# Keys and gates on one DMA queue, values on a second: a decode attention kernel with two load queues

## The chip, the cores and the metric

The kernel runs on one core of a Trainium2 chip. The metric is device microseconds of one execution, the median of several. The span on a profile page is about 1.8 us shorter than the device time of the same execution.

## The reference, cut to what matters

One new token for each of 4 batches meets a window of 4096 cached keys and values for 8 key/value heads of 128. A gated ReLU layer runs beside it, and a sigmoid gate mixes the two.

```python
k = jnp.repeat(k_cache[:, :, Sk - W:, :], rep, axis=1)      # W = 4096, rep = 4
v = jnp.repeat(v_cache[:, :, Sk - W:, :], rep, axis=1)
scores = jnp.einsum("bhqd,bhkd->bhqk", q, k) * (Dh ** -0.5)
p = _softmax(scores, axis=-1)
o = jnp.einsum("bhqk,bhkd->bhqd", p, v)
a = o.transpose(...).reshape(B, Sq, Hq * Dh) @ wo           # [...]
b = einsum(relu(x @ W_gate) * (x @ W_up), W_down)           # shortened
return g * a + (1 - g) * b                                  # g = sigmoid(sum(x * gate_w))
```

Everything in bfloat16. The data that has to be read is 81.01 MB: 33.6 MB of keys, 33.6 MB of values, 4.2 MB each of query and output weights, 1.8 MB each of gate, up and down weights. Every byte is used once, by few rows of activations.

## The kernel before

The profile calls TensorE PE, VectorE DVE, ScalarE ACT and SyncE, which here only issues DMAs, SP.

The work is cut into 8 sets (a batch and half of its heads). A set needs one K load and one V load of 4.19 MB each, 128 rows of 32 KB. Per set, VectorE transposes K in four blocks (KT) and takes the scores out of PSUM (ESC), TensorE multiplies scores (SC), VectorE transposes the exponents (PT), TensorE does a small product for the row maximum (SW), row sums (RS) and the value product (PV). ScalarE does the exponent (EXP) and the normalisation (NORM). At the end come gate and up products (GU), the down product (FFN), the fold of the heads (OQ) and the output product (WO).

All loads were issued by SP in one order, into four rotating slots (a slot is a buffer that holds one load):

```python
def _dma_order():
    o = [("wq",), ("x",), ("gw",), ("k", 0), ("k", 1), ("v", 0)]
    for s in range(2, NSET):
        o += [("k", s), ("v", s - 1)]
    return o + [("wg",), ("wu",), ("v", NSET - 1), ("wd",)] + [("wo", p) for p in range(len(WO_PIECES))]
```

The order of the engines' work, PE in particular, comes from one list:

```python
    for s in range(1, NSET):
        o += [("KT", s, 0), ("SC", s - 1, 3)] + [...] + [("SW", s - 1)]
        o += [("KT", s, 1), ("PT", s - 1), ("SC", s, 0), ("KT", s, 2), ("SC", s, 1), ("RS", s - 1), ("KT", s, 3)]
        o += [("SC", s, 2)] + [("PV", s - 1)] * (s < NSET - 1)
    s = NSET - 1
    o += [("SC", s, 3), ("SW", s), ("PV", s - 1), ("PT", s), ("RS", s), ("GU",), ("PV", s), ("FFN",), ("OQ", 1)]
    return o + [("WO", p) for p in range(len(WO_PIECES))]
```

The output product waits for its weights, for the folded heads, and for T2, because it accumulates in the PSUM bank that FFN's result was just read from:

```python
            w = [("WO", p), ("T2",)] + [("E", "OQ", g) for g in range(2)]
```

## Time and profile before

| | before |
|---|---|
| time, median of 3 runs | 197.7 us (197.62 to 197.79) |
| span of the profiled run | 196.2 us |
| bytes read, share of 16 DMA engines' span | 81.01 MB, 96.8% |
| VectorE waiting for keys, in all | 26.0 us |
| last output weights waited for until | 193.4 us |

These are lines of the page of the kernel before: two rows of the slices (40 equal slices of 4.9 us, tenths busy and GB/s), the DMA queue, and the chain that ended last.

```profile
DMA  6999999999999999999999999999999999999990
GB/s 220 441 415 428 456 448 441 418 429 428 434 441 434 434 424 434 428 428 428 428 428 428 424 428 428 441 423 441 418 448 428 434 409 440 429 409 419 420 386 30
...
q1 hardware_dynamic: 3904, 81.01, 96.8%
...
DMA 56%; DVE 32%; PE 7%; SPq 2%; issue 1%
```

The DMA engines are busy from the first slice to the last but one. 96.8% of 196.2 us is 189.9 us of packet time per engine, on average. The chain gives VectorE 32%, but VectorE also waits 26 us for keys: it is not the limit.

The next lines are the tail in the timeline of the kernel before. Columns: start in us, busy time in us, engine, line, operation, output and inputs; in brackets the idle time of the engine before it, and what ended that.

```profile
150.41 2.31 DVE L495 STREAM_TRANSPOSE kt<-slots 128x2048 f32<-128x2048 f32 x1 [4.67 <-DMA slots<-in_A_k_cache_dram]
...
169.35 2.00 ACT L603 ACTIVATE pe<-sc,negmax 128x2048 bf16<-128x2048 bf16 x1 [12.83 <-DVE negmax L532]
...
172.74 1.69 PE L314 MATMUL bank<-slots,xT 128*4 128x448 bf16 x32
...
179.24 5.33 PE L314 MATMUL bank<-slots,pT 128*64 128x512 bf16 x32 [4.81 <-DMA slots<-in_A_v_cache_dram]
...
184.50 1.69 PE L314 MATMUL bank<-slots,sc 128*4 128x256 bf16 x28
...
187.83 1.91 PE L314 MATMUL bank<-slots,oq 128*4 128x256 bf16 x32 [0.63 <-ACT oq L586]
190.90 1.04 PE L314 MATMUL bank<-slots,oq 128*4 128x256 bf16 x16 [1.16 <-DMA slots<-in_A_wo_dram]
...
193.42 0.38 PE L314 MATMUL bank<-slots,oq 128*4 128x256 bf16 x4 [0.26 <-DMA slots<-in_A_wo_dram]
```

Read from top to bottom: the keys of the last set (K7) are there at 150.4, its exponent starts at 169.4, gate and up products at 172.7. PV of the last set waits 4.8 us for V7; FFN starts as soon as PV has ended, at 184.5. Half of the 64 output matmuls are done by 189.7. From there on PE waits for output weights. The tail is bound by DMA: PE has slack before each of the last pieces.

### The profile page before, as it was taken

Reading aid. Unit: us, or ns where it says so; the run is one execution under the profiler, and the core shown is the slowest. Engines: PE = TensorE matmul, PEld = TensorE weight load, DVE = VectorE, ACT = ScalarE, POOL = GpSimd, SP = SyncE. Lnnn points to the kernel's source line nnn. Section 1 sums busy time; section 2 is a strip of 40 time slices with the busy share of each in tenths; the row PEclk is TensorE's granted clock in tenths of the full one; section 3 lists DMA queues with packets and bytes.
Section 4 is the critical chain, followed back from the end, with each engine's and each line's share of the span. In section 5 each row is a group of like instructions: output and inputs, shape, how many; then the busy total and the mean of one; then the engine's idle time right before and its main releaser. Section 6 shows DMA issues by size and latency. Waiting matters only on the chain.

```text
span 196.2 us, 1966 instructions
## 1 busy us (share of the span) xinstructions
PE 125.9 (64%) x784; PEld 56.3 (29%) x784; DVE 127.7 (65%) x192; ACT 30.7 (16%) x66; POOL 14.1 (7%) x38
## 2 busy tenths in 40 slices
PE   0029377584964874787589855965696449754964
PEld 0014223131422321242134422422242123322641
DVE  6105969999499819982997299729973996370000
ACT  2003420040131013001300240014001400420100
POOL 7776000000000000000000000000000000000000
PEclk9999759999999998899579969997999996997899
DMA  6999999999999999999999999999999999999990
GB/s 220 441 415 428 456 448 441 418 429 428 434 441 434 434 424 434 428 428 428 428 428 428 424 428 428 441 423 441 418 448 428 434 409 440 429 409 419 420 386 30
DMA packets 3922, 81.14 MB, mean 414 GB/s; under 512 B 572, under 2 KB 584, under 8 KB 968
## 3 DMA queue, kind: packets, MB, share of 16 engines
q1 hardware_dynamic: 3904, 81.01, 96.8%
q8 instruction: 6, 0.10, 0.2%
q14 instruction: 4, 0.03, 0.0%
q10 hardware_dynamic: 8, 0.00, 0.0%
HBM read 81.01 MB, written 0.00 MB: 413 GB/s over the span
## 4 chain that ended last, share of the span: by engine, by line
DMA 56%; DVE 32%; PE 7%; SPq 2%; issue 1%
DMA slots<-in_A_k_cache_dram 47%; DVE kt L495 21%; DMA slots<-in_A_wo_dram 9%; PE bank L314 7%; DVE sc L520 5%; DVE pT L536 5%; SPq L247 2%; DVE rd L526 1%; DVE rowmax L524 0%; DVE hmax L531 0%; DVE negmax L532 0%; DVE osum L560 0%; DVE recip L541 0%
## 5 line engine op out<-in xcount | busy, mean ns | idle before, releaser
L495 DVE STREAM_TRANSPOSE kt<-slots 128x2048 f32<-128x2048 f32 x32 | 73.6, 2302 | 26.1 <-DMA slots<-in_A_k_cache_dram 26.0
L314 PE MATMUL bank<-kt,qblk 128*128 128x512 bf16 x256 | 70.8, 423 | 21.7 <-DVE kt L495 21.7
L314 PEld LDWEIGHTS bank<-kt,qblk 128*128 128x128 bf16 x256 | 24.7, 104 | 59.6 <-DVE kt L495 26.1
L314 PE MATMUL bank<-slots,pT 128*64 128x512 bf16 x256 | 30.8, 396 | 4.8 <-DMA slots<-in_A_v_cache_dram 4.8
L603 ACT ACTIVATE pe<-sc,negmax 128x2048 bf16<-128x2048 bf16 x8 | 16.0, 2002 | 55.8 <-DVE negmax L532 55.8
L520 DVE TENSOR_SCALAR_CACHE_REDUCE sc<-bank 128x512 bf16<-128x512 f32 x32 | 21.0, 655 | 4.4 <-PE bank L314 4.4
L314 PEld LDWEIGHTS bank<-slots,pT 128*64 128x64 bf16 x256 | 14.9, 114 | 19.9 <-issue 9.3
L536 DVE STREAM_TRANSPOSE pT<-pe 128x2048 bf16<-128x2048 bf16 x8 | 18.5, 2312 | 2.2 <-ACT pe L603 2.2
L580 ACT ACTIVATE osb<-bank,recip 128x512 bf16<-128x512 f32 x8 | 5.5, 687 | 77.6 <-PE bank L314 77.6
L314 PE MATMUL bank<-rd,grpb 128*128 128x8 bf16 x8 | 1.5, 182 | 22.4 <-DVE rd L526 22.4
L314 PE MATMUL bank<-maskr,maskl 128*128 128x512 bf16 x32 | 13.0, 408 | 0.0
L318 PE MATMUL bank<-identb,xsb 4*128 4x4 bf16 x4 | 0.3, 173 | 13.4 <-DMA xsb<-in_A_x_dram 13.4
L314 PEld LDWEIGHTS bank<-rd,grpb 128*128 128x128 bf16 x8 | 0.8, 98 | 26.0 <-DVE rd L526 26.0
L556 DVE TENSOR_SCALAR t<-bank,gg 128x256 f32<-128x256 f32 x1 | 0.5, 484 | 10.1 <-PE bank L314 10.1
L314 PE MATMUL bank<-slots,oq 128*4 128x256 bf16 x64 | 4.3, 272 | 2.3 <-DMA slots<-in_A_wo_dram 1.6
L499 DVE COPY xT<-bank 128x16 bf16<-128x16 bf16 x1 | 0.2, 168 | 8.2 <-PE bank L318 8.2
L314 PE MATMUL bank<-slots,xT 128*4 128x512 bf16 (+1 forms) x64 | 5.3, 489 | 0.0
L560 DVE SCALAR_TENSOR_TENSOR osum<-bank,gg,t 128x256 bf16<-128x256 f32 x1 | 0.5, 484 | 7.1 <-PE bank L314 7.1
L314 PEld LDWEIGHTS bank<-maskr,maskl 128*128 128x128 bf16 x32 | 3.3, 103 | 4.8 <-issue 1.6
L482 DVE COPY qblk<-bank 32x32 bf16<-32x32 bf16 x32 | 4.0, 179 | 1.1 <-PE bank L318 0.9
L318 PEld LDWEIGHTS bank<-identb,xsb 4*128 4x128 bf16 x4 | 0.2, 114 | 13.4 <-DMA xsb<-in_A_x_dram 13.4
L577 ACT ACTIVATE qblk<-bank 32x32 bf16<-32x32 bf16 x32 | 3.5, 179 | 2.7 <-PE bank L318 2.6
(53 smaller groups left out, 60.7 us busy)
## 6 DMA issues: line engine op xcount, KB each, us to landing
slots<-in_A_k_cache_dram SPq DMA_DIRECT2D x8, 4096.0 KB, 24.7
slots<-in_A_v_cache_dram SPq DMA_DIRECT2D x8, 4096.0 KB, 31.5
slots<-in_A_wq_dram SPq DMA_DIRECT2D x1, 4096.0 KB, 12.4
slots<-in_A_wo_dram SPq DMA_DIRECT2D x3, 1024.0 KB, 15.5
slots<-in_B_W_gate_dram SPq DMA_DIRECT2D x1, 1792.0 KB, 19.9
slots<-in_B_W_up_dram SPq DMA_DIRECT2D x1, 1792.0 KB, 23.8
slots<-in_B_W_down_dram SPq DMA_DIRECT2D x1, 1792.0 KB, 18.8
slots<-in_A_wo_dram SPq DMA_DIRECT2D x1, 512.0 KB, 17.4
```

The costliest lines, as they stand in the source:

```text
L247: E.op(lambda: e.dma_start(dst, src), ev=ev, waits=waits, ctr=ctr)
L314: E.op(lambda: t.matmul(out_, lhsT, rhs, start=start, stop=stop, tile_position=pos, skip_group_check=True), ev=ev, waits=waits)
L318: E.op(lambda: t.transpose(out_, in_, idn), ev=ev, waits=waits)
L482: E.op(lambda dst=dst, r=r, g=g, e=e, src=src: copy(dst, src[r, g, 0:B, e, :, :]), ev=("E",) + key if (q, g, e) == (3, 1, 1) else None, wa ...
L495: E.op(lambda: v.transpose(kt[:, f, :].bitcast(FP32), slot("k", s)[:, 4096 * f:4096 * f + 4096].bitcast(FP32)), ev=("E", "KT", s, f), waits=w)
L520: E.op(lambda: v.tensor_scalar(sc[:, 512 * f:512 * f + 512], banks[scb(key)], 1.0, None, op0=ALU.mult, op1=ALU.max, accum_out=mx4[:, f:f + ...
L526: E.op(lambda: v.tensor_scalar(rd8[:, :], R["own8"][:, :], rowmax[:, 0:1], None, op0=ALU.mult), ev=("MAX", s), waits=[("RMX", s), ("OWN", ...
L536: E.op(lambda: v.transpose(pT[:, s % 2, :], pe[:, :]), ev=("E", "PT", s), waits=[("EXP", s)] + ([("PV", s - 2)] if s >= 2 else []))
L556: E.op(lambda: v.tensor_scalar(t2[:, :], banks[ACC][:, 0:OW], gg[:, 1:2], None, op0=ALU.mult), ev=("T2",), waits=[("FFN",), ("G",)])
L577: eqt(E, lambda d, x: a.activation(d, x, ACTF.Copy), n)
L580: E.op(lambda: a.activation(osb[:, s % 4, :], ob(s), ACTF.Copy, scale=recip[:, s % 2:s % 2 + 1]), ev=("NORM", s), waits=[("E", "RS", s), ( ...
L603: E.op(lambda: a.activation(pe[:, :], sc[:, :], ACTF.Exp, bias=negmax[:, s % 2:s % 2 + 1], scale=SCALE, accum_out=rowsum[:, s % 2:s % 2 + ...
```

## The change

Its intent: keys and values should arrive at the same time and not one after the other. K, gate, up and down weights stay on SP, V goes to the ACT queue, output weights are split over both. K has two slots, V has two. PV of set s-1 moves ahead of score block 2, so that a V slot comes free earlier. In the cut, `at` names the slot of a load and `wait` what must have ended before it is issued; `act` says after which piece of ScalarE's work a load is issued (EQT copies the queries).

```diff
-WO_PIECES = ((0, 8), (8, 16), (16, 24), (24, 28), (28, 30), (30, 32))
+WO_PIECES = ((0, 8), (8, 16), (21, 27), (16, 19), (27, 30), (19, 21), (30, 32))
+WO_ON_ACT = (0, 1, 3, 5)
 ...
-        o += [("SC", s, 2)] + [("PV", s - 1)] * (s < NSET - 1)
+        o += [("PV", s - 1), ("SC", s, 2)]
     s = NSET - 1
-    o += [("SC", s, 3), ("SW", s), ("PV", s - 1), ("PT", s), ("RS", s), ("GU",), ("PV", s), ("FFN",), ("OQ", 1)]
+    o += [("SC", s, 3), ("SW", s), ("PT", s), ("RS", s), ("GU",), ("PV", s), ("FFN",), ("OQ", 1)]
 ...
+    sp = [("wq",), ("x",), ("gw",)] + [("k", s) for s in range(NSET)] + [("wg",), ("wu",), ("wd",)]
+    sp += [("wo", p) for p in range(len(WO_PIECES)) if p not in WO_ON_ACT]
+    act = {("EQT", 1): [("v", 0), ("v", 1)]}
     for s in range(2, NSET):
-        o += [("k", s), ("v", s - 1)]
+        act[("NORM", s - 2)] = [("v", s)]
+    act[("NORM", NSET - 2)] = [("wo", p) for p in WO_ON_ACT]
+    return sp, act
 ...
+    for s in range(NSET):
+        at[("k", s)], at[("v", s)] = s % 2, 2 + s % 2
+        if s >= 2:
+            wait[("k", s)], wait[("v", s)] = [("E", "KT", s - 2, 3)], [("PV", s - 2)]
+    at[("wg",)] = at[("wu",)] = 0
+    wait[("wg",)] = wait[("wu",)] = [("E", "KT", NSET - 2, 3)]
+    at[("wd",)], wait[("wd",)] = 2, [("PV", NSET - 2)]
 ... (loader shared by the two queues, stop flag of the last output matmul)
```

More of the change, by code (lines that the diff above doesn't have):

```diff
@@ L143, in _order @@
         o += [("KT", s, 1), ("PT", s - 1), ("SC", s, 0), ("KT", s, 2), ("SC", s, 1), ("RS", s - 1), ("KT", s, 3)]
-        o += [("SC", s, 2)] + [("PV", s - 1)] * (s < NSET - 1)
+        o += [("PV", s - 1), ("SC", s, 2)]
     s = NSET - 1
-    o += [("SC", s, 3), ("SW", s), ("PV", s - 1), ("PT", s), ("RS", s), ("GU",), ("PV", s), ("FFN",), ("OQ", 1)]
+    o += [("SC", s, 3), ("SW", s), ("PT", s), ("RS", s), ("GU",), ("PV", s), ("FFN",), ("OQ", 1)]
     return o + [("WO", p) for p in range(len(WO_PIECES))]
 def _dma_order():
-    o = [("wq",), ("x",), ("gw",), ("k", 0), ("k", 1), ("v", 0)]
+    sp = [("wq",), ("x",), ("gw",)] + [("k", s) for s in range(NSET)] + [("wg",), ("wu",), ("wd",)]
+    sp += [("wo", p) for p in range(len(WO_PIECES)) if p not in WO_ON_ACT]
+    act = {("EQT", 1): [("v", 0), ("v", 1)]}
     for s in range(2, NSET):
-        o += [("k", s), ("v", s - 1)]
-    return o + [("wg",), ("wu",), ("v", NSET - 1), ("wd",)] + [("wo", p) for p in range(len(WO_PIECES))]
+        act[("NORM", s - 2)] = [("v", s)]
+    act[("NORM", NSET - 2)] = [("wo", p) for p in WO_ON_ACT]
+    return sp, act
 def _slots():
-    frees = [[] for _ in range(NSLOT)]
     at, wait = {}, {}
-    turn = 0
-    for it in _dma_order():
-        k = it[0]
-        if k in ("x", "gw") or (k == "wo" and it[1] > 0):
-            continue
-        if k == "wu":
-            at[it] = at[("wg",)]
-            wait[it] = wait[("wg",)]
-            continue
-        n = turn % NSLOT
-        turn += 1
-        at[it] = n
-        wait[it] = list(frees[n])
-        frees[n] = {"k": [("E", "KT", it[-1], 3)], "v": [("PV", it[-1])], "wq": [("Q", 1)], "wg": [("GU", 1)], "wd": [], "wo": []}[k]
+    for s in range(NSET):
+        at[("k", s)], at[("v", s)] = s % 2, 2 + s % 2
+        if s >= 2:
+            wait[("k", s)], wait[("v", s)] = [("E", "KT", s - 2, 3)], [("PV", s - 2)]
+    at[("wq",)], wait[("v", 1)] = 3, [("Q", 1)]
+    at[("wg",)] = at[("wu",)] = 0
+    wait[("wg",)] = wait[("wu",)] = [("E", "KT", NSET - 2, 3)]
+    at[("wd",)], wait[("wd",)] = 2, [("PV", NSET - 2)]
+    for p in range(len(WO_PIECES)):
+        at[("wo", p)], wait[("wo", p)] = 1, [("E", "KT", NSET - 1, 3)]
     return at, wait
@@ L241, in store, with loads @@
              ev=("OUT", t), waits=[("OSUM",)], ctr=f"d_out{t}")
-    def sync(e):
-        E = _Eng(plan, e, "sp")
+    def loads(E, e, items):
         def load(ev, ctr, dst, src, waits=()):
             E.op(lambda: e.dma_start(dst, src), ev=ev, waits=waits, ctr=ctr)
-        for it in _dma_order():
+        for it in items:
             k = it[0]
@@ L262, in sync @@
             elif k == "wd":
-                load(("WD",), "d_wd", Wd, B_W_down.rearrange("(p i) c -> p (i c)", i=14),
-                     waits=w)
+                load(("WD",), "d_wd", Wd, B_W_down.rearrange("(p i) c -> p (i c)", i=14), waits=w)
             elif k == "wo":
@@ L273, in sync @@
                      waits=w)
+    def sync(e):
+        E = _Eng(plan, e, "sp")
+        loads(E, e, _dma_order()[0])
         for t in range(0, OUTT, 2):
@@ L415, in WO @@
             lo, hi = WO_PIECES[p]
+            last = (len(WO_PIECES) - 1, WO_PIECES[-1][1] - 1)
             w = [("WO", p), ("T2",)] + [("E", "OQ", g) for g in range(2)]
@@ L418, in WO @@
                 for j in range(OUTT):
-                    mm(banks[ACC][OR * j:OR * j + 4, 0:OW], oq[:, i, :], Wo[:, i, OW * j:OW * j + OW], i == 0, i == 31,
+                    mm(banks[ACC][OR * j:OR * j + 4, 0:OW], oq[:, i, :], Wo[:, i, OW * j:OW * j + OW], i == 0, (p, i) == last,
                        ev=("WOP", p) if (i, j) == (hi - 1, OUTT - 1) else None, waits=w if (i, j) == (lo, 0) else (),
@@ L608, in scalar @@
             fns[it[0]](*it[1:])
+            loads(E, a, _dma_order()[1].get(it, []))
         for t in range(1, OUTT, 2):
```

## The prediction

> **What bounds the kernel now.** The DMA engines. The page's queue part gives queue q1 81.01 MB and 96.8% of 16 engines' span: 0.968 x 196.2 = 189.9 us of packet time per engine. The slices show DMA at 9 tenths almost throughout, mostly 415 to 440 GB/s. In the timeline the first load is issued at 0.8 us and the last output-weight piece is waited for until 193.4 us, so only about 3 us of this is not transfer. The chain of waits says DMA 56%, DVE 32%, but that DVE share is slack: the DVE needs about 14.6 us per set (four kt transposes of 2.2, four evictions of 0.6, one pT transpose of 2.25, about 1.3 of small steps), while one K plus one V load, 8.39 MB at about 428 GB/s, takes 19.6 us. VectorE waits 26.0 us for keys (list of waits). After the last piece come 0.4 us of PE, 0.5 us of DVE and about 2 us of store.
>
> **What the change does.** It removes no byte and practically no compute; one DMA is added. V moves to the ACT queue, output weights go to both, the rest stays on SP. The Trainium skill ("Trainium Kernel Development and Optimization", Key Constraints) says both queues run on the same 16 engines and interleave, so only issue time can be saved; the trace shows issue is not the limit (0.3 to 0.7 us per DMA, under transfers of 9.8 us). I expect no more bandwidth: q1's 189.9 us get divided, the sum unchanged within 1 us.
>
> Ordering costs in the middle should vanish in slack. V0 is issued only after the ACT query copies (about 25.9 us); K1 then shares and lands near 38 instead of 33 us. K2 is issued at about 35. From there both queues always have a load waiting (the next K is requested about 14 us after the previous K's landing, each takes 19.6 us shared). PV before score block 2 (PV is 3.6 us) ends that block about 0.2 us later than now.
>
> **The tail decides.** I estimate from these rates: K7 lands at about 156 us (now 150.4); V7, 32 KB rows against 14 KB gate rows, at 177 us if the engines alternate row by row (now 179.2), at 185 if bytes are shared equally, at 174 if whole loads alternate. The skill ("DMA: Bandwidth & Descriptors", Queues, rings and completion order) says each engine round-robins between queues by packet; the before trace, with one queue, cannot show it. Up weights then land near 180, down weights near 187 (now before 184.5, where FFN starts). GU 1.7, PV 3.6 to 5.3, FFN 1.7, OQ 1.1 plus its ACT copy 0.5, then 64 output matmuls at 0.06 = 3.8 us: FFN ends at about 189, OQ copy at 191, output matmuls at 194.7 instead of 193.8. Today half of them are done before 190; then they are bunched behind the DMA. That is +0.9 us; +3.7 us for equal bytes; about -0.3 for whole loads.
>
> **Prediction.** 198.3 us, 8 in 10 between 196.9 and 200.5. Faster by over 2%: 0.02; within 2%: 0.88; slower by over 2%: 0.10.
>
> **What would show it.** Two queue lines, SP about 42 MB and ACT about 39 MB, shares adding to about 97%; slices still 9; K and V landing about 20 us of transfer apart rather than 10; V0 issued near 26 us on ACT; VectorE's wait for keys as long in all; output matmuls starting at 189 to 191 instead of 187.8.
>
> **What would make it wrong.** Packet time changing when two rings feed one engine; a slot wait that empties both queues; V7 or down weights much later than 187 us, so that FFN, OQ and output matmuls lie bare after the last transfer (slower by 2%); the queues ending unevenly.

## The result and the profile after

| | before | after |
|---|---|---|
| time, median of 4 runs each | 197.75 us (197.62 to 197.81) | 198.69 us (198.47 to 198.89) |
| span of the profiled run | 196.2 us | 197.0 us |
| share of 16 engines' span, both queues | 96.8% | 96.4% |
| VectorE waiting for keys | 26.0 us | 24.5 us |
| first transpose of the last keys | 150.4 us | 157.7 us |
| output matmuls end | 193.8 us | 194.6 us |

The ratio of the times is 1.0048 (95% interval 1.0031 to 1.0066). Ratios are the mean time of one kernel's runs over that of the other's of the same rounds, so not quite the ratio of the medians. The change is slower by half a per cent, which is "same" at the 2% mark and yet clear of the noise.

From the page of the kernel after, the lines that answer to those of before:

```profile
DMA  6999999999999999999999999999999999999980
GB/s 220 446 427 452 434 439 439 422 427 432 426 426 432 426 426 422 432 432 439 439 439 432 429 427 426 439 432 432 429 432 426 422 420 437 417 409 426 415 335 9
...
q1 hardware_dynamic: 2320, 44.70, 53.4%
q10 hardware_dynamic: 1736, 36.31, 43.0%
...
DMA 65%; DVE 23%; PE 9%; SPq 1%; issue 1%; ACT 0%
```

53.4% and 43.0% of 197.0 us are together 189.9 us of packet time per engine, the same as one queue needed. Two queues have moved the same bytes through the same engines in the same time. This agrees with the Trainium skill ("Trainium Kernel Development and Optimization", Key Constraints): the queues share the 16 DMA engines.

The tail in the timeline of the kernel after:

```profile
157.73 2.31 DVE L497 STREAM_TRANSPOSE kt<-slots 128x2048 f32<-128x2048 f32 x1 [3.43 <-DMA slots<-in_A_k_cache_dram]
...
171.48 0.33 SPq L245 DMA_DIRECT2D slots<-in_B_W_down_dram  x1
...
177.31 2.00 ACT L605 ACTIVATE pe<-sc,negmax 128x2048 bf16<-128x2048 bf16 x1 [5.08 <-DVE negmax L534]
...
179.77 3.02 PE L315 MATMUL bank<-slots,xT 128*4 128x448 bf16 x32
...
182.72 3.95 PE L315 MATMUL bank<-slots,pT 128*64 128x512 bf16 x32
...
187.65 1.69 PE L315 MATMUL bank<-slots,sc 128*4 128x256 bf16 x28 [0.98 <-DMA slots<-in_B_W_down_dram]
189.27 1.08 PE L315 MATMUL bank<-osb,fold 128*64 128x128 bf16 x16
...
190.98 3.66 PE L315 MATMUL bank<-slots,oq 128*4 128x256 bf16 x64 [0.63 <-ACT oq L588]
```

The list of DMA issues gives the landings (engine, KB each, us from issue to landing):

```profile
slots<-in_A_v_cache_dram ACTq DMA_DIRECT2D x1, 4096.0 KB, 24.1
...
slots<-in_B_W_up_dram SPq DMA_DIRECT2D x1, 1792.0 KB, 27.9
slots<-in_B_W_down_dram SPq DMA_DIRECT2D x1, 1792.0 KB, 16.0
```

The last keys are there 7.3 us later than before, and the last exponent starts 8.0 us later (177.3 against 169.4). PV(7) no longer waits for V7; it is later because its own inputs are, and because GU before it took 3.02 us instead of 1.69: the granted clock was 0.74 between 179 and 181 us and 0.50 between 181 and 183, and its weight loads waited 0.30 us for the up weights. FFN waits a last 0.98 us for the down weights, which were issued at 171.5 and landed 16.0 us later. And all 64 output matmuls stand in one row of 3.66 us, with no wait for output weights: each is there before its turn. The end is no longer set by the last transfer: between 193 and 195 us the DMA share is 0.00, and PE ends 0.8 us later than before.

How the engines share their time between the queues can be read off the packet counts. The queue lines of the kernel after, in a window where both queues carry 32 KB rows (100 to 140 us):

```profile
q10 hardware_dynamic: 296, 8.59, 50.0%
q1 hardware_dynamic: 293, 8.55, 49.7%
```

and in one where V7 in 32 KB rows meets gate and up weights in 14 KB rows (162 to 172 us):

```profile
q10 hardware_dynamic: 96, 3.15, 73.1%
q1 hardware_dynamic: 95, 1.13, 27.1%
```

The counts are nearly equal in both; the bytes are not. Tiny completion packets are counted too: 16 of the 95 in the second window, and they take turns like rows. Between 162 and 168 us, where there are none, 52 rows of V7 (66.0%) stand against 55 gate rows (30.9%). Both queues move in every 2 us of this stretch (17 to 18 packets against 16 to 20), so it is not whole loads that take turns. The engines take one row of one queue, then one of the other, and the queue with longer rows gets more of the bandwidth.

### The profile page after: what moved, and what is told of

Its sections match the earlier page's. It is cut to its first block, busy times and chain, and to the rows that moved or that the text cites. A ratio compares the mean times of both kernels' runs of the same rounds, so it can differ in the third digit from the quotient of the medians.

```text
span 197.0 us, 1975 instructions
## 1 busy us (share of the span) xinstructions
PE 129.8 (66%) x784; PEld 58.6 (30%) x784; DVE 128.4 (65%) x192; ACT 30.7 (16%) x66; POOL 14.0 (7%) x38
## 3 DMA queue, kind: packets, MB, share of 16 engines
q1 hardware_dynamic: 2320, 44.70, 53.4%
q10 hardware_dynamic: 1736, 36.31, 43.0%
## 4 chain that ended last, share of the span: by engine, by line
DMA 65%; DVE 23%; PE 9%; SPq 1%; issue 1%; ACT 0%
DMA slots<-in_A_k_cache_dram 57%; DVE kt L497 15%; PE bank L315 9%; DMA slots<-in_B_W_down_dram 8%; DVE pT L538 3%; DVE sc L522 3%; SPq L245 1%; DVE rd L528 0%; DVE rowmax L526 0%; DVE hmax L533 0%; DVE osum L562 0%; DVE negmax L534 0%; ACT oq L588 0%; DVE recip L543 0%
## 5 line engine op out<-in xcount | busy, mean ns | idle before, releaser
L497 DVE STREAM_TRANSPOSE kt<-slots 128x2048 f32<-128x2048 f32 x32 | 73.6, 2302 | 24.5 <-DMA slots<-in_A_k_cache_dram 24.5
L315 PE MATMUL bank<-kt,qblk 128*128 128x512 bf16 x256 | 76.2, 448 | 3.6 <-DVE kt L497 3.6
L315 PEld LDWEIGHTS bank<-kt,qblk 128*128 128x128 bf16 x256 | 26.7, 109 | 46.1 <-issue 22.3
L315 PE MATMUL bank<-slots,pT 128*64 128x512 bf16 x256 | 29.5, 383 | 1.5 <-DMA slots<-in_A_v_cache_dram 1.5
L315 PEld LDWEIGHTS bank<-slots,pT 128*64 128x64 bf16 x256 | 14.3, 111 | 13.7 <-issue 2.7
L315 PE MATMUL bank<-maskr,maskl 128*128 128x512 bf16 x32 | 13.5, 423 | 0.0
L315 PE MATMUL bank<-slots,xT 128*4 128x512 bf16 (+1 forms) x64 | 6.7, 591 | 0.0
L315 PE MATMUL bank<-slots,oq 128*4 128x256 bf16 x64 | 3.7, 272 | 0.6 <-ACT oq L588 0.6
L315 PEld LDWEIGHTS bank<-rowsum,grpf 128*128 128x128 f32 x16 | 2.9, 187 | 3.7 <-ACT pe L605 2.7
L315 PE MATMUL bank<-rowsum,grpf 128*128 128x1 f32 x16 | 2.3, 214 | 2.6 <-ACT pe L605 2.6
## 6 DMA issues: line engine op xcount, KB each, us to landing
slots<-in_B_W_up_dram SPq DMA_DIRECT2D x1, 1792.0 KB, 27.9
```

The lines of the kernel that those rows point to most:

```text
L315: E.op(lambda: t.matmul(out_, lhsT, rhs, start=start, stop=stop, tile_position=pos, skip_group_check=True), ev=ev, waits=waits)
L497: E.op(lambda: v.transpose(kt[:, f, :].bitcast(FP32), slot("k", s)[:, 4096 * f:4096 * f + 4096].bitcast(FP32)), ev=("E", "KT", s, f), waits=w)
```

## The experiments

My theory at the start: the loss is all in the tail, where down weights, FFN, fold and output matmuls stand bare at the end. Rivals: the PE order costs time; two queues slow each other; the granted PE clock, which fell from 0.922 to 0.861, stretches the work. Two kept traces of the changed kernel already speak on the clock: before FFN, PE stands idle for the down weights (0.98 us here, 1.75 us in the control below), and from 187 to 194 us its granted clock is 1.00 in both. PE's clock does not directly set the end of these two runs. The first four runs shared one chip, where before took 197.70 us.

### e1: the PE order alone

```diff
 (on the kernel before)
-        o += [("SC", s, 2)] + [("PV", s - 1)] * (s < NSET - 1)
+        o += [("PV", s - 1), ("SC", s, 2)]
-    o += [("SC", s, 3), ("SW", s), ("PV", s - 1), ("PT", s), ...
+    o += [("SC", s, 3), ("SW", s), ("PT", s), ...
```

> The kernel before with only the PE order changed (PV ahead of score block 2), one DMA queue as before. My theory (the loss is the bare tail after the late down weights, and PV order costs only slack): 197.7 us, within 0.3 of before. Rival (PV in front of score block 2 holds up VectorE's last scores and that is what cost the 0.9 us): about 198.6.

Measured: 197.74 us, ratio 0.9993 (0.9981 to 1.0005). As my theory expected. PV ahead of score block 2 costs nothing here, and this kernel runs at a mean clock of 0.852 to 0.878, as low as the changed one, without being slower (its tail still waits for DMA, so this alone does not clear the clock). In its timeline the last keys are used from 150.66 on, as before:

```profile
150.66 2.31 DVE L495 STREAM_TRANSPOSE kt<-slots 128x2048 f32<-128x2048 f32 x1 [3.16 <-DMA slots<-in_A_k_cache_dram]
```

The PE order does not make them late; what is left of the change is the queues, with the load order and the slots that go with them.

### e2: the queues with the old PE order

```diff
 (on the kernel after)
-        o += [("PV", s - 1), ("SC", s, 2)]
+        o += [("SC", s, 2)] + [("PV", s - 1)] * (s < NSET - 1)
-    o += [("SC", s, 3), ("SW", s), ("PT", s), ...
+    o += [("SC", s, 3), ("SW", s), ("PV", s - 1), ("PT", s), ...
```

> The changed kernel with the PE order of before (PV after score block 2, and behind the last switch in the last set). My theory: PV(6) ends near 179 us instead of 171.4, so the down weights and the ACT output weights are issued at 179 to 180 instead of 171.5 to 172; V7 has landed at 175.7 and the up weights end near 178, so both queues run empty for about 2 us, seen as a dip of the DMA row near 179 us, and the time is 200 to 201. Rival (PV order alone costs the 0.9 us): 197.7, faster than the change.

Measured: 202.60 us (201.53 to 203.54), ratio 1.024. Two stretches of its profiled run, which at 201.53 us was the fastest (columns: window, its length, busy us of PE, PE load, VectorE, ScalarE and GpSimd with instruction counts, granted clock, DMA share, GB/s):

```profile
170.00:176.00 6.00, 4.75 (x23) 1.93 (x23) 3.03 (x9) 0.28 (x1) 0.00 (x0) 0.85 0.99 421
176.00:180.00 4.00, 4.00 (x50) 2.04 (x50) 2.15 (x1) 2.50 (x3) 0.00 (x0) 1.00 0.31 104
```

and its timeline:

```profile
178.91 0.33 SPq L245 DMA_DIRECT2D slots<-in_B_W_down_dram  x1
...
188.69 3.00 PE L315 MATMUL bank<-slots,sc 128*4 128x256 bf16 x28 [4.32 <-DMA slots<-in_B_W_down_dram]
```

Between 176 and 180 us the engines are 31% busy: 2.8 us are lost, for the reason expected: everything that is left to load waits for PV(6), and PV(6) now comes last. FFN then waits 4.3 us for the down weights. The loss is larger than I wrote (up to 203.5 and not 201): in the profiled run FFN's 3.00 us instead of 1.69 at full rate, and the fold's 1.39 instead of 1.08, come on top. What the slower runs add, no trace shows. So moving PV is free with one queue and necessary with two.

### e3: all output weights on SP

```diff
-WO_ON_ACT = (0, 1, 3, 5)
+WO_ON_ACT = ()
```

> The changed kernel with all output weights on SP, behind the down weights. My theory: nothing shares with up and down weights once V7 has landed (175.7), so up weights land near 179, down weights near 183 instead of 187.5; FFN follows PV(7) at once, output matmuls start near 189.8 and end near 193.6, with the last transfer landing at 193.0 as always: 197.6 to 197.9. Rival (two queues as such slow the transfers, or a lower PE clock costs the time): no better than 198.7.

Measured: 198.32 us (197.53 to 199.37), ratio 1.0038 (1.0012 to 1.0064). Half of it came true: in the profiled run (197.75 us) the down weights land 11.8 us after their issue at 171.3, so at 183.1 instead of 187.5; FFN follows PV(7) at 186.4, and the output matmuls start at 189.8. The line of its DMA issues:

```profile
slots<-in_B_W_down_dram SPq DMA_DIRECT2D x1, 1792.0 KB, 11.8
```

But the runs spread over 1.8 us, against 0.4 us for the change itself. Taking away one wait did not take away the loss: another string stands right behind it. The interval overlaps that of the change, so the size of the gain is uncertain. PE's clock is part of this string: GU took 3.09 us and held up PV(7) until 182.63, while its input pT was ready at 181.59, so by these figures an estimated 1.0 us comes from PE below full rate. No run isolates it.

### e4: V7 in two loads of 16 KB rows

```diff
 (V7 only)
-load(..., slot("v", 7), rows)
+load(..., slot("v", 7)[:, 0:8192], rows[:, :, 0:8192])
+load(..., slot("v", 7)[:, 8192:16384], rows[:, :, 8192:16384])
```

> The changed kernel with only V7 loaded as two transfers of 16 KB rows instead of one of 32 KB rows. Same bytes, one more DMA. If the engines alternate row by row: V7's share against the 14 KB gate rows falls from 70 to 53%, V7 lands about 7 us later (182 to 183), up weights about 4 us earlier (176 to 177), down weights about 3 us earlier (184 to 185); PV(7) starts no later than now (182.7), FFN no longer waits, about 197.8. If bytes or whole loads are shared: landings move by under 1 us and the time stays 198.7.

Measured: 198.44 us (197.77 to 200.60), ratio 1.0049 (1.0013 to 1.0085). The queue lines of this run in a window where V7 meets the 14 KB rows (164 to 174 us):

```profile
q10 hardware_dynamic: 155, 2.28, 53.8%
q1 hardware_dynamic: 150, 1.92, 45.6%
```

The same bytes, cut into rows of half the length, get 53.8% of the engines instead of 73.1%. The alternation row by row is shown, and the down weights land at 170.4 + 14.3 = 184.7 us, as expected. The time of the profiled run (198.03 us) was near the one expected, the median was not: the spread is 2.8 us, and again one wait gone brought little.

### The control, and a guess at the clock

The next four shared another chip (before: 197.69 us).

> The changed kernel unchanged, as a control beside the next three on one chip. 198.7 us. If the lower PE clock costs time here (the tail from the last score block to the output product is bound by PE and not by DMA), its runs with the lower mean clock are the longer ones, as in the runs with output weights on SP (197.5 us at 0.869 to 199.4 at 0.853); the kernel before, bound by DMA at its end, shows no such order.

Measured: 198.79 us (198.67 to 199.11), ratio 1.0059 (1.0046 to 1.0072). The loss repeats. The order by clock does not: 0.870 gave 198.67, 0.853 gave 198.70 and 198.79, 0.861 gave 198.84, 0.862 gave 199.11. For this kernel the mean clock of a run doesn't predict its time; for the variants without the wait for the down weights it is different, as shown under e3 below.

Then half of the score matmuls of sets 3 to 6 were left out, with a wrong result:

```diff
                     for e in range(2):
+                        if 3 <= s <= 6 and e == 1:
+                            continue
```

> Wrong result on purpose: the changed kernel with half of the score matmuls of sets 3 to 6 left out (64 of 784 matmuls), nothing changed in set 7 and in the tail, no load changed. If the lower clock of PE, brought on by its work before, stretches the tail: mean clock rises to 0.92 or more, the last sets' and tail's matmuls run at full rate, time 197.9 to 198.3 with less spread. If the clock doesn't matter: 198.7 as the control.

Measured: 198.70 us (198.25 to 199.29), ratio 1.0051, at a mean clock of 0.818 to 0.835. The clock went down with less PE work, not up, so the run did not produce the condition that it was to test. It shows only that PE work in the middle sets isn't what sets the time. No run here isolates why the clock fell.

### e5 and e6: giving keys precedence

All V loads in two halves of 16 KB rows, so that K gets two thirds of the rate; e6 also has all output weights on SP.

```diff
-                load(("V", s), ..., slot("v", s), rows)
+                load(("VA", s), ..., slot("v", s)[:, 0:8192], rows[:, :, 0:8192])
+                load(("V", s), ..., slot("v", s)[:, 8192:16384], rows[:, :, 8192:16384])
```

> The changed kernel with every V load as two transfers of 16 KB rows, K as before in 32 KB rows: the same bytes. If the engines alternate row by row, K gets two thirds of the rate while both run: K runs ahead to its slot limit, K7 lands near 140 us instead of 157.7, V7 near 178, VectorE's work on the last keys is done before V6 and V7 land, PV(7) starts near 179 and the tail follows the DMA again: 197.7 to 197.9 with a spread under 0.5 us. If late keys are not the cause of the tail bound by compute: no better than 198.7, with a spread of 1 us or more.

> As the run with all V in halves, and all output weights on SP behind the down weights. My theory: the down weights land about 2 us earlier still, but nothing waits for them any more, so the same 197.7 to 197.9. If the output weights on ACT are a cause of their own: faster than the run with V in halves by 0.5 us or more.

Measured: e5 199.11 us (198.28 to 200.80), ratio 1.0077; e6 198.50 us (198.30 to 199.84), ratio 1.0055. My expectation fell for e5. For e6 the medians differ from e5 by 0.61 us, more than the 0.5 us that I had named as the sign that output weights on ACT cost time of their own; but the intervals (1.0047 to 1.0108 and 1.0033 to 1.0078) overlap, so this stays open. Two lines of the waits in e5 (engine and line, what it waited for, us in total, times, the longest):

```profile
DVE sc L526 <- remote: 31.9, 6, 8.7
...
PE bank L319 <- DMA slots<-in_A_v_cache_dram: 22.2, 6, 6.5
```

Keys now come early (K7 lands 19.9 us after its issue at 130.4, so at 150.3, though not at 140), but PE waits 22.2 us for values (1.5 us in the changed kernel). PV(s-1) stands in front of score block 2 on PE, and a late V(s-1) holds up the scores of the next set, and VectorE behind them (the releaser shown as "remote" was not resolved by the profile). The last set's transposes begin at 157.4 us, no earlier than in the changed kernel. Shifting bandwidth from values to keys only changes which of the two the last set waits for.

### e7: the tail's PE order and a PSUM bank of its own

```diff
-... ("GU",), ("PV", s), ("FFN",), ("OQ", 1)]
+... ("GU",), ("PV", s), ("OQ", 1), ("FFN",)]
-            w = [("WO", p), ("T2",)] + [("E", "OQ", g) for g in range(2)]
+            w = [("WO", p)] + [("E", "OQ", g) for g in range(2)]
 (output product and its last read: banks[ACC] -> banks[OB[0]])
```

> The changed kernel, loads untouched, with the tail's PE order alone changed: the output product accumulates in a PSUM bank of its own, so it need not wait for FFN's result to be read, and the fold of the last heads (OQ) goes ahead of FFN. Down weights still land near 187.4. If the loss is the string down weights, FFN, fold, copy, 64 output matmuls behind each other: fold runs at 186.6 to 187.6, FFN 188 to 189.7, output matmuls start at 189.8 instead of 190.9 and end near 193.5: 197.6 to 198.0. If it is anything earlier than the tail: 198.7.

Measured, with before at 197.63 us: 198.06 us (197.70 to 198.74), ratio 1.0031 (1.0014 to 1.0048). The timeline of its profiled run (197.70 us):

```profile
186.39 1.08 PE L315 MATMUL bank<-osb,fold 128*64 128x128 bf16 x16 [0.84 <-ACT osb L582]
187.40 1.69 PE L315 MATMUL bank<-slots,sc 128*4 128x256 bf16 x28
...
188.93 2.90 PE L315 MATMUL bank<-slots,oq 128*4 128x256 bf16 x50
...
192.31 1.26 PE L315 MATMUL bank<-slots,oq 128*4 128x256 bf16 x14 [0.49 <-DMA slots<-in_A_wo_dram]
```

No load was touched; the down weights landed at 187.2 as in the change (issued at 170.3, 16.9 us to landing). The output matmuls start 2 us earlier, and PE waits for output weights again: the end is back at the DMA. This trace is of the fastest of six runs; but five of the six are faster than the fastest of the nine runs of the changed kernel (198.47 us, on other chips). So the string of work after the down weights is shown to be a cause. Shortening it recovers a part of the loss: the median stays 0.4 us above before.

### e3 three more times: what the spread is

> All output weights on SP, as run before (197.5 to 199.4), for its spread and another trace. There the chain ended through score, exponent, GU, PV, FFN, fold and output matmuls without a DMA. If PE's half-rate stretches set its length, a longer run shows GU (1.7 at full rate), PV (3.6) or FFN (1.7) stretched by the same amount as its end is late, and the down weights landing by 184 as ever. If DMA sets it: the down or output weights land later by that amount.

> The same kernel once more, one look: time and trace beside the others; the difference from the other looks should be the PE half-rate stretches between 161 us and the end.

> The same kernel a third time in this call, as the one before: 197.5 to 199.4, the difference explained by GU, PV or FFN at half rate, not by a later landing.

Measured: 198.21 us (197.69 to 199.16), ratio 1.0035; the looks took 197.71 and 197.91 us. The profiled run of the first happened to be its longest. The quick look, 197.71 us:

```profile
157.56 2.31 DVE L497 STREAM_TRANSPOSE kt<-slots 128x2048 f32<-128x2048 f32 x1 [4.25 <-DMA slots<-in_A_k_cache_dram]
...
176.85 2.00 ACT L605 ACTIVATE pe<-sc,negmax 128x2048 bf16<-128x2048 bf16 x1 [5.08 <-DVE negmax L534]
...
186.08 1.69 PE L315 MATMUL bank<-slots,sc 128*4 128x256 bf16 x28
...
193.09 0.38 PE L315 MATMUL bank<-slots,oq 128*4 128x256 bf16 x4 [0.23 <-DMA slots<-in_A_wo_dram]
```

The long run of the same kernel, 199.16 us:

```profile
158.81 2.31 DVE L497 STREAM_TRANSPOSE kt<-slots 128x2048 f32<-128x2048 f32 x1 [3.54 <-DMA slots<-in_A_k_cache_dram]
...
178.75 2.00 ACT L605 ACTIVATE pe<-sc,negmax 128x2048 bf16<-128x2048 bf16 x1 [5.08 <-DVE negmax L534]
...
188.04 1.69 PE L315 MATMUL bank<-slots,sc 128*4 128x256 bf16 x28
...
191.37 3.66 PE L315 MATMUL bank<-slots,oq 128*4 128x256 bf16 x64 [0.63 <-ACT oq L588]
```

The long run is 1.25 us behind when its last keys come (158.81 against 157.56), 1.90 at the exponent, 1.96 at FFN. Of the 0.65 us added between keys and exponent, one group of score matmuls accounts for 0.66: in the timeline it took 2.92 us instead of 2.26, in a stretch of reduced clock. The second look (197.91 us) shows both terms apart: its keys come at 158.01, 0.45 behind the quick one, but its exponent only 0.14 behind, as its scores ran faster. The down weights land at 183 in both (171.01 + 12.0 and 172.92 + 10.2). So I was half right: the spread isn't from the late weights, but neither is it from GU, PV or FFN. Between these two runs two thirds of it is the landing of the last keys (K7 was issued at 133.19 against 131.86), and the rest the clock during the scores. Why K7 was issued later is not shown. The quick run has caught up with the DMA at its end (0.23 us of waiting for output weights), the long one has not.

In e3 (both sets), e4 and e7, where FFN did not wait for the down weights in the trace, the eleven timed runs with a mean clock of 0.861 or more took 197.53 to 198.25 us, the thirteen with 0.853 or less 198.06 to 200.60 us. So here a lower clock does go with a longer run, and it may be what keeps these medians above before. Whether the clock stretches the run, or late data lower the clock, no run here shows.

## Why the prediction was right, point by point

Predicted 198.3 us, measured 198.69; the stated range held it.

| step | predicted | measured |
|---|---|---|
| packet time per engine | 189.9 us, unchanged | 189.9 us |
| V0 issued on ACT | 25.9 us | 24.9 us |
| K7 lands | 156 us | 157.7 us |
| V7 lands (row by row) | 177 us | 151.6 + 24.1 = 175.7 us |
| up weights land | near 180 us | 152.9 + 27.9 = 180.8 us |
| down weights land | near 187 us | 171.5 + 16.0 = 187.5 us |
| FFN ends | 189 us | 187.65 + 1.69 = 189.3 us |
| output matmuls end | 194.7 us | 190.98 + 3.66 = 194.6 us |
| SP and ACT megabytes | 42 and 39 | 44.70 and 36.31 |

- The engines as the bound, and no gain from two queues: right, on every page.
- The sharing: of the three ways offered, row by row held. V7's share of 73.1% in 32 KB rows and 53.8% in 16 KB rows, with nearly equal packet counts, shows it.
- The tail's cost: +0.9 us was written for row by row, and the median moved by +0.94. The headline 198.3 was lower; the prediction doesn't say how it weighed its three cases. That +0.9 and +0.94 agree so closely is partly luck: K7 came 1.7 us later than predicted and GU took 3.02 us instead of 1.7, and both were hidden only because the down weights came another 0.98 us later.
- The order of PE in the middle costing nothing: right with one queue (e1).
- The split of megabytes was simply added up wrongly: 8 V loads of 4.19 MB and 21/32 of the output weights make 36.3 MB, not 39. No time rested on it.
- What the prediction missed: it named the down weights as the wait to fear. e3 removed that wait, and got only a third to a half of the loss back, by the medians. The string of compute from the last keys (157.7 us) to PV(7) (ending 186.7) ended just 1 us before the down weights, so two things end the tail nearly together. Before, that string started at 150.4 and had slack. Single runs of e3 and e7 reached 197.5 to 197.9, the level of before; their medians did not.

What stays open: how much of the loss in e3, e4 and e7 is PE's clock, why the mean clock fell when PE had less to do (e8), and how to bring the last set forward with two queues; e5 shows that precedence for keys alone does not. No version here beats the kernel before: e1 equals it, and their spans of 195.6 to 196.4 us lie only some 6 us above the 189.9 us of packets.

## What to carry to other kernels

With the DMA engines already busy all the time, a second queue brought no bandwidth here (189.9 us of packet time with one and with two); what it changed is who arrives when. In these traces the queues took turns row by row, so the length of the rows acted as the priority. Compare, for the last block of work, when its inputs land and how long the string behind them is: with one queue the order of loads is under your control, and with two the string can become the new end. Removing a single wait from such a tail is worth only the distance to the next one.

## What the Trainium skill lacked or had wrong

- "DMA: Bandwidth & Descriptors", section Queues, rings and completion order, says that an engine drains a whole packet, typically about 9 to 17 descriptors, from one queue before it switches. One V load puts 8 rows and a completion on each engine; read so, I took it to mean that whole loads could alternate. The runs show single rows alternating: 52 rows of V7 (1.70 MB) against 55 gate rows (0.79 MB) between 162 and 168 us. What the profile calls a packet is here one row of the load, or one completion.
- The same page draws no consequence for bandwidth: a queue's share went with its row length. V7 had 73.1% of the engines in 32 KB rows against 14 KB rows, and 53.8% in 16 KB rows.
- "Trainium Kernel Development and Optimization", Key Constraints, was right that queues share the engines (189.9 us of packet time with one queue and with two), but issuing from two did not "only" save issue time: with the load order and slots that came with it, it moved the landing of the last keys by 7.3 us.
